# Attention and two MLPs on one core: the rotated q and k split in fewer VectorE steps, and new numbers for the planner

## The chip, the cores and the metric

The kernel runs on one core of one Trainium2 chip. The metric is the time of the whole program on the device in microseconds; the median of three runs before the change is 1078.23 us (1077.92 to 1079.2). Engines are named as the profile names them: PE is TensorE (PEld its weight loads), DVE is VectorE, ACT is ScalarE, POOL is GpSimd, SP is SyncE, whose queue issues the kernel's DMAs.

## The reference

Attention with rotary positions over four batches of eight heads, 576 tokens and a head size of 64, then two dense MLPs over the 2304 tokens (512 to 2048 to 512), the first with x times sigmoid(1.702 x), the second with ELU:

```python
q_rot, k_rot = rotate(q), rotate(k)
scores = (1 / sqrt(D)) * q_rot @ k_rot.T          # (4, 8, 576, 576)
attn = softmax(scores)                            # exp(s - max) / (sum + 1e-9)
x = (attn @ v) in rows of tokens                  # (2304, 512)
h = x @ w_in;  x = (h * sigmoid(1.702 * h)) @ w_out
h = x @ w_in2; out = where(h > 0, h, exp(min(h, 0)) - 1) @ w_out2
```

All inputs are float32 (the weights come as 64-bit numbers that the kernel itself turns into float32).

## The kernel before

Every product is made from two float16 halves. A float32 value is scaled by a power of two, its high half is the value rounded to float16, its low half is what remains. A product takes three matmuls in the MLPs (high times high, high times low, low times high). For the scores, one column of the transposed q holds 64 high and 64 low values of a head, and the first matmul takes it against the high values of k twice over, the second against the low values of k over the high half of q and zeros over the low one: two matmuls in place of three.

The work goes by head pairs: 4 batches times 4 pairs are 16 preparations (`prep`, lines 597 to 709). One of them loads q and k of two heads into the only buffer `R`, takes their largest magnitudes (`amax`), spreads them over the partitions through PE (`across`, lines 354 and 364), makes the scales (`scale`, line 621), rotates (`rope_swap`, `rope_cos`, `rope_add`: lines 634, 638, 642), writes the high halves on ACT (`k_hi`, `q_hi`: lines 656, 662) and the low halves on DVE (`low`, line 667: one instruction for each head), all into the float16 tile `n16`, and transposes that tile with one DMA into `qkT` (line 684). `scale` makes, in DVE steps of two columns, the limited maximum, its exponent bits, the scale `qk_s` and the inverse `qk_i` (lines 336, 338, 340), and the factor of the scores `qk_c` as inverse times inverse times 1/8 (line 626).

A unit of scores is 128 queries of one head (or 64 of two): matmuls (line 798), the maximum on DVE (802), small steps (806, 817, 821), the exponential on ACT (810), the high half on ACT, sometimes on DVE (826, 830), the low half on DVE (838), and a transposing DMA into `et` (844, 847). There are 144 units. When a block of 256 or 320 tokens of a head pair has its transposes, PE multiplies by v (`av`, line 990), ACT and DVE write the halves of `x` (993, 997).

The first MLP (`first_mlp`, lines 1036 and 1070) runs over 8 such blocks; a block can begin when `x` of its four head pairs is there. The second MLP (lines 1177 and 1218) follows when all of the first is done. The weights are turned into float32 in steps on ACT and DVE (lines 424 to 443, the choice of engine free for some), measured (457), and split into halves (500 to 524).

What sets the order is a planner, `Plan.run`: each operation has keys, costs by engine, operations that it must follow and buffers that it needs; each planned engine takes the ready operation with the smallest key, and the instructions are written out in that order for each engine's queue. The keys come from the table `TUNE`; `f_dve` and `f_act` are offsets that bias operations that may run on either engine. MLP work has keys far behind all attention work, so that it fills what PE has left. A switch table `FLEX` holds variants that are off (a form of attention without transposes, `fast_unit`, whose constants are made at the start all the same).

Of the kernel before, what the change touches and what calls it, by code (L numbers as in the profile page):

```python
# [16 lines left out]
P = 128  # L17


FLEX = dict(  # L20
    Ehi=1, Elo=0, glo=0, qk=0, pE=0, pW=0, pg=0, dg=0, r0=1, r1=1, r2=0, r3=0, nt0=0, nt1=0, nt2=0, nt3=0,
)
# [4 lines left out]
    pe_w1i=12, pe_w1o=0, lsame=218.42826132665004, tab=-72.97, f_dve=158.19, f_act=8.42, f_pool=12.224437399728332,  # L27
    w2s=195.33, w1i2=50.4, w1o2=-142.64, dlat=823.3988909607715, qh=-59.5,
    kt=-32.02, vam=131.57, p0=1, lat=344.9241913205742, slack=1000000000.0, w1i=-51.38,
    w1i_s=2.9, w1o=59.09, w1o_s=1.19, prep0_s=0.45, nt=5.6622832505119804,  # L30
    s_f=40.3256386921686, mx_f=6.7540349396707375, ex_f=7.075547533776429, av_f=14.806376760777082, prep0=49.34,
    prep=-60.31, va0=-39.21, va=-62.78, vs=0.59, tiny=2.79,
    av=4.76, ex=-62.15, mx=-22.0, s=-24.23, tr=-61.89,
    bits=-42.89,
# [190 lines left out]
def kernel(  # L225
# [90 lines left out]
    buf("V", ap_, [P, 650], F32, BUFS["V"])  # L316
    buf("mr", ap_, [6, 256], BF16, BUFS["mr"])
# [68 lines left out]
    class Weight:  # L386
        def __init__(self, tile_fn, src, wide, tag, rbuf, key, after=()):
# [107 lines left out]
            for i, c in enumerate(seq):  # L495
                ks = key(16 + i) + TUNE.get(tag + "2", 0.0)

                def hi(e, c=c, i=i):
                    if e == "act":
                        nc.scalar.activation(out=self.h[:, self.at[c], 0:512], in_=self.t[:, i + SP, :], func=AF.Copy, scale=self.sc["s"])  # L500
                    elif e == "pool":
                        nc.gpsimd.tensor_scalar(out=self.h[:, self.at[c], 0:512], in0=self.t[:, i + SP, :], scalar1=self.sc["s"], scalar2=1.0, op0=ALU.mult, op1=ALU.mult)
                    else:
                        nc.vector.tensor_scalar(out=self.h[:, self.at[c], 0:512], in0=self.t[:, i + SP, :], scalar1=self.sc["s"], scalar2=None, op0=ALU.mult)
# [5 lines left out]
                o2 = op({"act": c_act(512, ptr=1), "dve": c_dve(512, 2, ptr=1), **({"pool": 750} if FLEX["pW"] else {})}, hi, [so, free.get(i)], ks, port=True)  # L510
# [63 lines left out]
    def light(e):  # L574
        for a in range(2):
            nc.gpsimd.memset(n16[:, 4 + a, :, D - D * a:2 * D - D * a], 0.0)
        nc.gpsimd.memset(ones, 1.0)
        nc.gpsimd.memset(line, 0.0)
        nc.gpsimd.memset(line[:, D:D + 1], 1e-9)
        nc.gpsimd.memset(square, 1.0)  # L580

    def consts(e):
        nc.gpsimd.tensor_scalar(out=minus, in0=eye, scalar1=-1.0, scalar2=1.0, op0=ALU.mult, op1=ALU.mult)
        nc.gpsimd.tensor_scalar(out=eye16, in0=eye, scalar1=1.0, scalar2=1.0, op0=ALU.mult, op1=ALU.mult)
        nc.vector.tensor_reduce(out=pick_c, in_=eye[0:6, 0:6].rearrange("p (a s) -> p a s", a=2), axis=AX.X, op=ALU.add)
        for a in range(2):
            nc.gpsimd.tensor_scalar(out=pick[:, a], in0=eye[0:6], scalar1=0.0, scalar2=pick_c[:, a:a + 1], op0=ALU.mult, op1=ALU.add)
# [3 lines left out]
    ready_c = op({"pool": 1400}, consts, [begin], key=TUNE["tab"])  # L591
# [5 lines left out]
    def prep(b, hp):  # L597
# [46 lines left out]
        def q_parts():  # L644
            f = take(hN).rearrange("p x j c -> p (x j c)")
            hi = f[:, 0:2 * 704].rearrange("p (h r) -> p h r", h=2)[:, :, 0:640].rearrange("p h (j c) -> p h j c", c=P)[:, :, :, 0:D]
            lo = f[:, D:D + 2 * 576].rearrange("p (h g d) -> p h g d", h=2, g=9)[:, :, 0:9:2]
            return hi, lo

        def k_parts():  # L650
            N16 = take(hN)
            hi = N16[:, 2:4].rearrange("p x j (u d) -> p (x j) u d", u=2)
            return hi, N16[:, 2:4, :, 0:D], [N16[:, 4 + a, :, D * a:D * a + D] for a in range(2)]

        def k_hi(e):
            nc.scalar.activation(
                out=k_parts()[0], in_=R5()[:, 1].rearrange("p h j d -> p (h j) d").unsqueeze(2).to_broadcast([P, 10, 2, D]),
# [3 lines left out]
        def q_hi(e):  # L661
            nc.scalar.activation(out=q_parts()[0], in_=R5()[:, 0], func=AF.Copy, scale=st["s"][:, 0:1])

        def low(e, t, dst, hi):
            for h in range(2):
                if e == "dve":
                    nc.vector.scalar_tensor_tensor(out=dst[h], in0=R5()[:, t, h], scalar=st["s"][:, t:t + 1], in1=hi[:, h], op0=ALU.mult, op1=ALU.subtract)  # L667
                else:
                    nc.gpsimd.tensor_tensor(out=dst[h], in0=R5()[:, t, h], in1=hi[:, h], op=ALU.subtract)

# [650 lines left out]
```

## Time and profile before

| | us |
|---|---|
| median of 3 runs | 1078.23 |
| profiled execution, whole time | 1078.97 |
| its span | 1077.2 |
| PE busy | 964.2 |
| DVE busy | 791.0 |
| ACT busy | 655.0 |

The page gives sums of busy time by engine; PE's share is 90%. A share over the whole says little here, for the stages differ: the attention stage loads all engines, and in the second MLP DVE and ACT wait for PE for long times. The views by stretches and by waits are read for that reason.

### The profile page before, as it was taken

The numbers are of one execution on the slowest core, as the hardware profiler recorded it, in microseconds if no ns is written. First come the engines' busy times: TensorE is split into PE (matmuls) and PEld (weight loads), VectorE is DVE, ScalarE is ACT, GpSimd is POOL, SyncE is SP. The second block draws the span as 40 slices with busy tenths as digits, with TensorE's granted clock in tenths as the row PEclk, the third lists the DMA queues.
The fourth block names the chain that finished last, engine by engine and source line by source line (L and its number), as shares of the span: only waits on it lengthen the run. The fifth ranks groups of instructions, "written<-read, shape, count | busy, mean of one in ns | idle before, by whom it ended". The sixth has DMA issues, their size and how long they took to land.

```text
span 1077.2 us, 18378 instructions
## 1 busy us (share of the span) xinstructions
PE 964.2 (90%) x6710; PEld 612.2 (57%) x6710; DVE 791.0 (73%) x1886; ACT 655.0 (61%) x1277; POOL 8.2 (1%) x31
## 2 busy tenths in 40 slices
PE   1366557999999999999999999999999999999998
PEld 0124325767776767866788778744444444444474
DVE  6998898989989989999895979898066056046051
ACT  5688987868878868877575749675044044035041
POOL 1000000000000000000000000000000000000000
PEclk9998758999999999999999999999999999999999
DMA  8989975488879677876865552711001100000000
GB/s 268 262 202 222 230 163 100 91 177 147 163 162 161 138 165 164 158 157 114 154 123 139 168 164 85 235 58 49 20 10 30 30 11 10 30 10 1 21 20 19
DMA packets 292314, 124.81 MB, mean 116 GB/s; under 512 B 264576, under 2 KB 279552, under 8 KB 292224
## 3 DMA queue, kind: packets, MB, share of 16 engines
q1 hardware_dynamic: 292224, 123.64, 50.6%
q8 instruction: 52, 0.85, 0.4%
q14 instruction: 38, 0.31, 0.1%
HBM read 53.35 MB, written 9.44 MB: 58 GB/s over the span
## 4 chain that ended last, share of the span: by engine, by line
PE 52%; DVE 25%; DMA 11%; ACT 5%; issue 3%; SPq 3%; POOL 0%; DVEq 0%; ACTq 0%; POOLq 0%
PE m L1218 16%; PE m L1177 14%; PE m L1070 9%; DMA et<-Ehl 6%; PE m L1036 6%; PE av L990 4%; DVE Ehl L838 3%; DMA R<-in_k_dram 3%; PE s L798 3%; DVE st L802 3%; DVE t L1043 2%; DVE gl L1053 2%; DVE n L667 2%; ACT E L810 1%; DVE T L634 1%
## 5 line engine op out<-in xcount | busy, mean ns | idle before, releaser
L1036 PE MATMUL m<-x,wi 128*128 128x320 f16 (+1 forms) x1536 | 198.1, 286 | 1.8 <-ACT y L1076 0.9
L1070 PE MATMUL m<-gh,wo 128*128 128x256 f16 (+1 forms) x1024 | 198.5, 286 | 0.0
L1218 PE MATMUL m<-w2o,g 128*128 128x512 f16 x864 | 189.1, 379 | 1.4 <-ACT w2o L500 0.8
L1177 PE MATMUL m<-yhl,w2i 128*128 128x512 f16 (+1 forms) x960 | 188.2, 358 | 2.2 <-DVE e L1188 2.1
L1036 PEld LDWEIGHTS <-wi 128*128 128x128 f16 x1536 | 148.7, 98 | 42.4 <-issue 5.4
L1070 PEld LDWEIGHTS <-wo 128*128 128x128 f16 x1536 | 148.5, 98 | 40.2 <-issue 3.5
L1177 PEld LDWEIGHTS <-w2i 128*128 128x128 f16 x960 | 93.7, 98 | 94.9 <-issue 2.9
L1070 PE MATMUL m<-gl,wo 128*128 128x320 f16 (+1 forms) x512 | 146.3, 286 | 0.0
L1218 PEld LDWEIGHTS <-g 128*128 128x128 f16 x864 | 84.1, 98 | 102.5 <-issue 2.7
L810 ACT ACTIVATE E<-s,st,qk_c 128x576 f32<-128x576 f32 x144 | 118.7, 825 | 23.4 <-DVE st L806 17.4
L798 PE MATMUL s<-qkT 128*128 128x288 f16 (+1 forms) x640 | 102.2, 310 | 27.1 <-ACT E L810 24.5
L838 DVE SCALAR_TENSOR_TENSOR Ehl<-E,st,Ehl 128x576 f16<-128x576 f32 x144 | 116.1, 810 | 10.6 <-ACT Ehl L826 10.1
L826 ACT ACTIVATE Ehl<-E,st 128x576 f16<-128x576 f32 x127 | 97.2, 770 | 36.1 <-DMA et<-Ehl 19.6
L1184 DVE TENSOR_SCALAR e<-e 128x512 f32<-128x512 f32 (+1 forms) x80 | 31.6, 395 | 113.8 <-ACT e L1180 113.8
L802 DVE TENSOR_REDUCE st<-s 128x1 f32<-128x576 f32 x144 | 106.0, 745 | 4.6 <-PE s L798 4.1
L1221 ACT ACTIVATE o<-m,eo 128x512 f32<-128x512 f32 x18 | 12.4, 688 | 158.3 <-PE m L1218 158.3
L798 PEld LDWEIGHTS <-qkT 128*128 128x128 f16 (+1 forms) x640 | 58.0, 105 | 65.3 <-issue 48.0
L1191 ACT ACTIVATE g<-e,y_c 128x512 f16<-128x512 f32 (+1 forms) x80 | 54.2, 677 | 57.5 <-DVE e L1188 57.1
L1195 DVE SCALAR_TENSOR_TENSOR g<-e,y_c,g 128x512 f16<-128x512 f32 (+1 forms) x80 | 55.5, 694 | 28.3 <-ACT g L1191 27.5
L1039 ACT ACTIVATE t<-m,hsc 128x320 f32<-128x320 f32 (+1 forms) x128 | 63.4, 496 | 10.2 <-PE m L1036 9.7
L1180 ACT ACTIVATE e<-m,y_c 128x512 f32<-128x512 f32 (+1 forms) x80 | 50.8, 635 | 22.6 <-PE m L1177 19.7
L1047 ACT ACTIVATE gh<-t 128x320 f16<-128x320 f32 (+1 forms) x128 | 55.5, 439 | 10.0 <-DVE t L1043 9.7
(162 smaller groups left out, 1104.9 us busy)
## 6 DMA issues: line engine op xcount, KB each, us to landing
R<-in_moe_w_in_dram SPq DMA_DIRECT2D x16, 512.0 KB, 4.2
R<-in_moe_w_out_dram SPq DMA_DIRECT2D x16, 512.0 KB, 4.4
gh<-in_moe_w_in_dram SPq DMA_DIRECT2D x8, 512.0 KB, 4.7
R<-in_q_dram SPq DMA_DIRECT2D x16, 256.0 KB, 2.7
R<-in_k_dram SPq DMA_DIRECT2D x16, 256.0 KB, 3.2
gl<-in_moe_w_in_dram SPq DMA_DIRECT2D x8, 512.0 KB, 5.0
V<-in_v_dram SPq DMA_DIRECT2D x32, 128.0 KB, 3.5
gh<-in_moe_w_out_dram SPq DMA_DIRECT2D x8, 512.0 KB, 4.5
```

The lines of the kernel that those rows point to most:

```text
L798: nc.tensor.matmul(o, X[:, a, t], X[:, 2 + 2 * x + a, cs], start=x == 0, stop=x == 1)
L802: nc.vector.tensor_reduce(out=st["t"][:, 0:1], in_=take(hS)[:, :, 0:NS], axis=AX.XY, op=ALU.max, negate=True)
L810: nc.scalar.activation(out=take(hE).rearrange("p (c f) -> p c f", c=2), in_=take(hS)[:, :, 0:NS], func=AF.Exp, bias=t[:, 1:2], scale=csc[b ...
L826: nc.scalar.activation(out=X16[:, 0:S], in_=take(hE), func=AF.Copy, scale=st["t"][:, 3:4])
L838: nc.vector.scalar_tensor_tensor(out=X16[:, S:2 * S], in0=E, scalar=r, in1=X16[:, 0:S], op0=ALU.mult, op1=ALU.subtract)
L1036: nc.tensor.matmul(ps[:, 0:N], W1i.lhs(kk, u, wl), x[:, xl, 0:N], start=kk == 0 and i == 0, stop=kk == KD - 1 and i == 2)
L1039: nc.scalar.activation(out=take(ht)[:, 0:N], in_=take(hM)[:, 0:N], func=AF.Tanh, scale=hsc[b][:, 1:2])
L1047: nc.scalar.activation(out=gh[:, u, 0:N], in_=take(ht)[:, 0:N], func=AF.Copy, scale=DOWN / 2)
L1070: nc.tensor.matmul(ps[:, 0:N], W1o.lhs(f, d, wl), (gh, gl)[xl][:, f, 0:N], start=f == 0 and i == 0, stop=f == KF - 1 and i == 2)
L1177: nc.tensor.matmul(ps[:, 0:n], W2i.lhs(kk, u, wl), Y[:, xl, kk, 0:n], start=kk == 0 and i == 0, stop=kk == KD - 1 and i == 2)
L1195: nc.vector.scalar_tensor_tensor(out=g[:, u, 512:512 + n], in0=take(he)[:, 0:n], scalar=st["c"][:, 1:2], in1=g[:, u, 0:n], op0=ALU.mult, o ...
L1218: nc.tensor.matmul(ps, g[:, f, 512 * gi + P * tt:512 * gi + P * tt + P], W2o.h[:, f, 512 * wl:512 * wl + 512], start=f == 0 and i == 0, st ...
```

## The change

Four things are edited.

- The low halves of q, and those of k, become one DVE instruction of 640 elements for both heads. For that the tile has new columns: both heads of q have their high half in columns 0 to 63 and their low half in 64 to 127, and the low half of k stands in columns 0 to 63 for both heads, with zeros in 64 to 127 (before, the second head had it the other way round).
- The factor of the scores is made by adding exponent bits as integers, from the masked maxima; the inverse scale of q and k is not made any more. The lower limit of the maxima is 2^-47 in place of 2^-60.
- The table of switches and the variants that were off are removed, with their constants (`eye16`, `pick`, `line`), and v's tile has rows of 64 values in place of 65.
- The planner gets other numbers: a smaller cost for the low halves and for `scale`, and most keys in `TUNE`.

```diff
@@ TUNE (two lines of it)
-    kt=-32.02, vam=131.57, p0=1, lat=344.9241913205742, slack=1000000000.0, w1i=-51.38,
+    kt=-23.72, vam=107.88, p0=1, lat=344.9241913205742, slack=1000000000.0, w1i=-85.68,
...
@@ light, consts
-        for a in range(2):
-            nc.gpsimd.memset(n16[:, 4 + a, :, D - D * a:2 * D - D * a], 0.0)
+        nc.gpsimd.memset(n16[:, 4:6, :, D:2 * D], 0.0)
...
-        nc.gpsimd.tensor_scalar(out=eye16, in0=eye, scalar1=1.0, scalar2=1.0, op0=ALU.mult, op1=ALU.mult)
-        nc.vector.tensor_reduce(out=pick_c, in_=eye[0:6, 0:6].rearrange("p (a s) -> p a s", a=2), axis=AX.X, op=ALU.add)
...
@@ scale
-            nc.vector.tensor_scalar(out=m, in0=take(hG)[:, 256:258], scalar1=TINY, scalar2=None, op0=ALU.max)
-            s, inv = scale_bits(m, 2, "qk", 8)
-            c = tiny(1, "qk_c", B * NP)
-            nc.vector.scalar_tensor_tensor(out=c, in0=inv[:, 0:1], scalar=1.0 / D ** 0.5, in1=inv[:, 1:2], op0=ALU.mult, op1=ALU.mult)
...
+            nc.vector.tensor_scalar(out=m, in0=take(hG)[:, 256:258], scalar1=2.0 ** -47, scalar2=None, op0=ALU.max)
+            x = tiny(2, "qk_x", 2, I32)
+            nc.vector.tensor_scalar(out=x, in0=m.bitcast(I32), scalar1=0x7F800000, scalar2=None, op0=ALU.bitwise_and)
+            s = st["s"] = tiny(2, "qk_s", 8)
+            nc.vector.tensor_scalar(out=s.bitcast(I32), in0=x, scalar1=-1, scalar2=268 << 23, op0=ALU.mult, op1=ALU.add)
+            c = csc[b, hp] = tiny(1, "qk_c", B * NP)
+            nc.vector.scalar_tensor_tensor(out=c.bitcast(I32), in0=x[:, 0:1], scalar=-(158 << 23), in1=x[:, 1:2], op0=ALU.add, op1=ALU.add)
...
@@ halves of q and k
+        def part(x, w):
+            return take(hN)[:, x:x + 2, :, D * w:D * w + D].rearrange("p x j d -> p (x j) d")
...
-        def low(e, t, dst, hi):
-            for h in range(2):
-                if e == "dve":
-                    nc.vector.scalar_tensor_tensor(out=dst[h], in0=R5()[:, t, h], scalar=st["s"][:, t:t + 1], in1=hi[:, h], op0=ALU.mult, op1=ALU.subtract)
...
+        def low(e, t):
+            nc.vector.scalar_tensor_tensor(
+                out=part(4 * t, 1 - t), in0=R5()[:, t].rearrange("p h j d -> p (h j) d"), scalar=st["s"][:, t:t + 1],
+                in1=part(2 * t, 0), op0=ALU.mult, op1=ALU.subtract,
+            )
...
-            kl = op({"dve": c_dve(640, k=2, ptr=2)}, k_lo, [kh], key, use=[hR, hN], port=True)
+        kl = op({"dve": c_dve(640, ptr=1)}, k_lo, [kh], key, use=[hR, hN], port=True)
...
@@ v
-    buf("V", ap_, [P, 650], F32, BUFS["V"])
+    buf("V", ap_, [P, 640], F32, BUFS["V"])
```

Where instructions stand now is shown at three places. In these rows `gh` and `gl` are buffers of raw weights, `wi` and `wo` the first MLP's weights, `R` the loaded q and k, `n` the float16 tile, `tab` the rotary table.

SyncE's queue at the program's start, before:

```order
L571 DMA eye<-in_rope_dram 128x128
L572 DMA tab<-in_rope_dram 128x640
L417 DMA gh<-in_moe_w_in_dram 128x1024
L610 DMA R_101<-in_q_dram 128x2x256
L611 DMA R_101<-in_q_dram 64x2x64
L610 DMA R_101<-in_k_dram 128x2x256
L611 DMA R_101<-in_k_dram 64x2x64
```

And after:

```order
L560 DMA eye<-in_rope_dram 128x128
L561 DMA tab<-in_rope_dram 128x640
L413 DMA gh<-in_moe_w_in_dram 128x1024 x2
L413 DMA gl<-in_moe_w_in_dram 128x1024 x2
L592 DMA R_103<-in_q_dram 128x2x256
L593 DMA R_103<-in_q_dram 64x2x64
L592 DMA R_103<-in_k_dram 128x2x256
L593 DMA R_103<-in_k_dram 64x2x64
```

Four loads of weights stand ahead of the first q and k where one stood.

DVE's queue at the first head pair's scale and low halves (`qk_m` to `n`), before:

```order
L623 TENSOR_SCALAR qk_m<-m_130 128x2
L336 TENSOR_SCALAR qk_b<-qk_m 128x2
L338 TENSOR_SCALAR qk_s<-qk_b 128x2
L340 TENSOR_SCALAR qk_i<-qk_b 128x2
L626 SCALAR_TENSOR_TENSOR qk_c<-qk_i 128x1
L642 TENSOR_TENSOR R_101<-R_101,T_121 128x1280
L438 SCALAR_TENSOR_TENSOR gh<-wi,gh 128x512
L438 SCALAR_TENSOR_TENSOR gl<-wi,gl 128x512
L443 SCALAR_TENSOR_TENSOR wi<-wi,gh 128x512
L667 SCALAR_TENSOR_TENSOR n_73<-R_101,qk_s,n_73 128x5x64 x2
L443 SCALAR_TENSOR_TENSOR wi<-wi,gl 128x512
L667 SCALAR_TENSOR_TENSOR n_73<-R_101,qk_s,n_73 128x5x64 x2
```

And after, the scale and what follows it, then (from the third row of the second piece) the low halves:

```order
L605 TENSOR_SCALAR qk_m<-m_146 128x2
L607 TENSOR_SCALAR qk_x<-qk_m 128x2
L609 TENSOR_SCALAR qk_s<-qk_x 128x2
L611 SCALAR_TENSOR_TENSOR qk_c<-qk_x 128x1
L434 SCALAR_TENSOR_TENSOR gh<-wi,gh 128x512
L621 TENSOR_TENSOR R_103<-R_103,tab 128x1280
```

```order
L434 SCALAR_TENSOR_TENSOR gl<-wi,gl 128x512
L439 SCALAR_TENSOR_TENSOR wi<-wi,gl 128x512
L640 SCALAR_TENSOR_TENSOR n_73<-R_103,qk_s,n_73 128x10x64
L429 TENSOR_SCALAR gh<-gh 128x512
L640 SCALAR_TENSOR_TENSOR n_73<-R_103,qk_s,n_73 128x10x64
```

The scale has four steps where it had five, the low halves two instructions where they had four, and more weight steps stand around them.

DVE's queue at the first GELU step of the first MLP (`t<-t,m`; `x` is a half of the attention's result, `Ehl` the halves of the probabilities), before:

```order
L634 TENSOR_TENSOR T_1276<-R_1232,tab 128x20x32
L997 SCALAR_TENSOR_TENSOR x_1512<-av_1468,x_1512 128x256
L508 SCALAR_TENSOR_TENSOR wo<-wo,w1o_s 128x512
L821 RECIPROCAL st<-st 128x1
L838 SCALAR_TENSOR_TENSOR Ehl_1515<-E_1457,st,Ehl_1515 128x576
L771 SCALAR_TENSOR_TENSOR v_1531<-V_697,v_s,v_1531 128x640
L1043 SCALAR_TENSOR_TENSOR t_1550<-t_1550,m_1517 128x320
```

And after:

```order
L502 SCALAR_TENSOR_TENSOR wo<-wo,w1o_s 128x512
L828 SCALAR_TENSOR_TENSOR x_1469<-av_1429,x_1469 128x256
L775 RECIPROCAL st<-st 128x1
L760 TENSOR_TENSOR st<-st,qk_c 128x1
L725 SCALAR_TENSOR_TENSOR v_1472<-V_481,v_s,v_1472 128x640
L502 SCALAR_TENSOR_TENSOR wo<-wo,w1o_s 128x512
L874 SCALAR_TENSOR_TENSOR t_1509<-t_1509,m_1474 128x320
```

The step keeps its neighbours: the sixth result of the attention (the second `x` of 256 columns) stands just ahead of it in both, and one unit of scores fewer stands ahead of it in the order after. PE's queue has the same instructions in both kernels, and its first MLP begins behind 33 units of scores in place of 34.

## Rows read from the trace of the kernel before

**Rows 1.** The page, first part: busy us, share of span, instructions, by engine

```profile
PE 964.2 (90%) x6710; PEld 612.2 (57%) x6710; DVE 791.0 (73%) x1886; ACT 655.0 (61%) x1277; POOL 8.2 (1%) x31
```

**Rows 2.** Busy time by engine in stretches of the span, with columns named

```profile
core 0: us, PE busy (x) PEld busy (x) DVE busy (x) ACT busy (x) POOL busy (x), PEclk, DMA share, GB/s
0.00:60.00 60.00, 14.97 (x108) 8.17 (x108) 49.10 (x104) 39.91 (x70) 3.71 (x18) 1.00 0.96 265
60.00:175.90 115.90, 72.44 (x418) 40.19 (x418) 102.22 (x267) 96.58 (x184) 1.46 (x3) 0.76 0.89 189
175.90:565.50 389.60, 372.55 (x3265) 281.54 (x3263) 357.63 (x958) 299.17 (x624) 3.06 (x10) 1.00 0.73 146
565.50:700.20 134.70, 134.70 (x1123) 106.75 (x1121) 112.58 (x227) 88.11 (x188) 0.00 (x0) 1.00 0.53 158
```

**Rows 3.** PE's waits, 175.9 to 565.5 us: total us, times, longest us

```profile
PE av L990 <- DMA et<-Ehl: 6.8, 8, 1.7
PE s L798 <- ACT E L810: 5.4, 12, 1.0
PE s L798 <- DMA qkT<-n: 2.3, 2, 1.2
```

**Rows 4.** Timeline of PE at the first MLP's start: start us, us, instructions

```profile
167.90 2.83 PE L990 MATMUL av<-et,v 128*64 128x320 f16 x19 [0.45 <-DMA et<-Ehl]
170.31 1.48 PE L990 MATMUL av<-et,vsh 128*64 128x320 f16 x8
173.13 0.65 PE L798 MATMUL s<-qkT 128*128 128x288 f16 x4 [1.34 <-ACT E L810]
...
175.36 0.66 PE L798 MATMUL s<-qkT 128*128 128x288 f16 x4
175.86 5.05 PE L1036 MATMUL m<-x,wi 128*128 128x320 f16 x36
```

**Rows 5.** Groups of DVE instructions by form: count, busy us, mean ns, idle before

```profile
L667 DVE SCALAR_TENSOR_TENSOR n<-R,qk_s,n 128x320 f16<-128x320 f32 x64 | 31.8, 542 | 0.4 <-ACT n L656 0.4
...
L771 DVE SCALAR_TENSOR_TENSOR v<-V,v_s,v 128x640 f16<-128x640 f32 x16 | 13.9, 874 | 0.0
...
L426 DVE TENSOR_SCALAR w2o<-R 128x512 f32<-128x512 f32 x4 | 1.7, 424 | 0.5 <-DMA R<-in_moe_w_out_dram 0.5
L619 DVE TENSOR_REDUCE am<-R 128x2 f32<-128x1280 f32 x1 | 1.5, 1478 | 0.0
...
L433 DVE TENSOR_SCALAR gh<-gh 128x512 int32<-128x512 int32 x2 | 0.9, 428 | 5.3 <-DMA gh<-in_moe_w_in_dram 5.3
...
L524 DVE CAST wi<-m 128x512 f16<-128x512 f32 x1 | 0.7, 673 | 0.0
...
L504 DVE TENSOR_SCALAR wi<-wi,w1i_s 128x512 f16<-128x512 f32 x1 | 0.5, 487 | 0.0
```

**Rows 6.** Timeline of DVE at one scale, one pair of low halves, v's low half

```profile
30.61 0.17 DVE L338 TENSOR_SCALAR qk_s<-qk_b 128x2 int32<-128x2 int32 x1
30.69 0.16 DVE L340 TENSOR_SCALAR qk_i<-qk_b 128x2 int32<-128x2 int32 x1
30.89 0.16 DVE L626 SCALAR_TENSOR_TENSOR qk_c<-qk_i 128x1 f32<-128x1 f32 x1
30.96 1.48 DVE L642 TENSOR_TENSOR R<-R,T 128x1280 f32<-128x1280 f32 x1
...
69.79 0.99 DVE L667 SCALAR_TENSOR_TENSOR n<-R,qk_s,n 128x320 f16<-128x320 f32 x2
70.71 0.14 DVE L806 TENSOR_TENSOR st<-st,qk_c 128x1 f32<-128x1 f32 x1
...
145.56 0.88 DVE L771 SCALAR_TENSOR_TENSOR v<-V,v_s,v 128x640 f16<-128x640 f32 x1
146.35 0.81 DVE L838 SCALAR_TENSOR_TENSOR Ehl<-E,st,Ehl 128x576 f16<-128x576 f32 x1
```

**Rows 7.** DMA issues by line: count, KB each, median us from issue to landing

```profile
gh<-in_moe_w_in_dram SPq DMA_DIRECT2D x8, 512.0 KB, 4.7
```

More of the change, by code (lines that the diff above doesn't have):

```diff
@@ L642, in rope_add @@
             ENG[e].tensor_tensor(out=R, in0=R, in1=take(hT).rearrange("p a j d -> p (a j d)"), op=ALU.add)
[L644 to L653, printed above, removed]
+        def part(x, w):
+            return take(hN)[:, x:x + 2, :, D * w:D * w + D].rearrange("p x j d -> p (x j) d")
         def k_hi(e):
             nc.scalar.activation(
-                out=k_parts()[0], in_=R5()[:, 1].rearrange("p h j d -> p (h j) d").unsqueeze(2).to_broadcast([P, 10, 2, D]),
+                out=take(hN)[:, 2:4].rearrange("p x j (u d) -> p (x j) u d", u=2), in_=R5()[:, 1].rearrange("p h j d -> p (h j) d").unsqueeze(2).to_broadcast([P, 10, 2, D]),
                 func=AF.Copy, scale=st["s"][:, 1:2],
@@ L661, in q_hi @@
         def q_hi(e):
-            nc.scalar.activation(out=q_parts()[0], in_=R5()[:, 0], func=AF.Copy, scale=st["s"][:, 0:1])
-        def low(e, t, dst, hi):
-            for h in range(2):
-                if e == "dve":
-                    nc.vector.scalar_tensor_tensor(out=dst[h], in0=R5()[:, t, h], scalar=st["s"][:, t:t + 1], in1=hi[:, h], op0=ALU.mult, op1=ALU.subtract)
-                else:
-                    nc.gpsimd.tensor_tensor(out=dst[h], in0=R5()[:, t, h], in1=hi[:, h], op=ALU.subtract)
-        def scaled(e, t):
-            x = take(hR)[:, 640 * t:640 * t + 640]
-            nc.gpsimd.tensor_scalar(out=x, in0=x, scalar1=st["s"][:, t:t + 1], scalar2=1.0, op0=ALU.mult, op1=ALU.mult)
+            nc.scalar.activation(out=part(0, 0), in_=R5()[:, 0].rearrange("p h j d -> p (h j) d"), func=AF.Copy, scale=st["s"][:, 0:1])
+        def low(e, t):
[3 more added lines that the diff above has]
+            )
         def k_lo(e):
-            _, hi, lo = k_parts()
-            low(e, 1, lo, hi)
+            low(e, 1)
         def q_lo(e):
-            hi, lo = q_parts()
-            low(e, 0, [lo[:, a] for a in range(2)], hi)
+            low(e, 0)
         def tr(e):
@@ L690, in prep @@
         rd = am_last[hp % 2] = across(lambda: am_t[hp % 2], 2, hG, [am], key)
-        sc = op({"dve": 720}, scale, [rd], key, use=[hG], port=True)
+        sc = op({"dve": 560}, scale, [rd], key, use=[hG], port=True)
         reng = lambda n: {"dve": c_dve(n)}
@@ L719 @@
     v_loaded = {}
-    n_fast = sum(FLEX[f"nt{hp}"] for hp in range(NP))
-    def fast(n, hp):
-        b, chunks, tail, n0, N = blocks[n]
-        return n == 0 and len(chunks) == 2 and not tail and FLEX[f"nt{hp}"]
     def v_view(b, hp):
-        return take(("vs", b, hp)).rearrange("p (a d) -> p a d", d=D + 1)
+        return take(("vs", b, hp)).rearrange("p (a d) -> p a d", d=D)
     def v_prep(b):
@@ L1257 @@
                 s_unit(i, trs, trs_st)
-            (fast_unit if fast(n, hp) else av_unit)(n, hp, trs, trs_st)
+            av_unit(n, hp, trs, trs_st)
     prev = None
```

155 lines of the change are left out of this document (13 added, 142 removed).

## The prediction, made before the changed kernel ran

> **What bounds the kernel now.** I read the page's engine totals first [rows 1]: PE is busy for 964.2 of the span's 1077.2 us, DVE for 791.0, and only 113.0 us of the span are without a matmul. Totals hide the stages, so the next view is the table by stretches [rows 2], cut at 175.9 us, where PE takes up the first MLP's first matmul [rows 4]. PE's idle time there is stretch minus busy: 60.0 - 15.0 = 45.0 us in the first 60 us, 115.9 - 72.4 = 43.5 us up to 175.9, 389.6 - 372.6 = 17.0 us up to 565.5, and none from 565.5 to 700.2. That leaves 113.0 - 105.5 = 7.5 us for the second MLP, which the change doesn't reach except by its weight steps. So the end is "start of the first MLP on PE, plus a fixed amount of PE work, plus the stalls behind it". The change leaves PE's instructions as they are, the same forms and counts. Only two terms can move: when the first MLP starts (call it A0), and the 17.0 us of stalls between A0 and 565.5.
>
> What sets A0? The PE rows ahead of it [rows 4] show no wait at 175.86. It stands in PE's order behind two score steps and another unit's attention product; the last operand that its own block lacked came out of the attention product that went on at 167.90, after a wait for the transposed probabilities, and ended at 170.31 + 1.48 = 171.8. Those probabilities come through DVE (maximum, reciprocal, low half), and DVE is busy for 49.1 of the first 60 us and 102.2 of the next 115.9 [rows 2]: idle 10.9 + 13.7 = 24.6 us in 175.9. (PE's granted clock is 0.76 of full between 60 and 175.9 us and 1.00 behind; with 43.5 us idle there PE isn't the limit at either level, and the change gives no reason for another one behind A0.) DVE's work ahead of A0 is therefore the thing to count. Behind A0 the picture turns: PE 96% busy, DVE 357.6 of 389.6 us (92%), and PE's waits are for the probabilities' transposes, 6.8 us, for ScalarE's exponentials that free a score buffer, 5.4 us, and for the transposed q and k, 2.3 us [rows 3]. The first two end in a chain through DVE too, so less DVE work can shorten them, but no further than their sum.
>
> **The merged low halves.** Before, the low half of q or k is two instructions of 320 elements, 64 in all, 542 ns each [rows 5]. They are pipelined: a pair that begins at 69.79 lets the next instruction start at 70.71, 0.92 us on [rows 6]. After, one instruction of 640 elements. The nearest row is v's low half: same operation, types and size, 874 ns [rows 5], and the instruction behind it starts 146.35 - 145.56 = 0.79 us on [rows 6]. Gain 0.13 us a pair, 0.26 us for each of the 16 head pairs. The new output is strided (64 of every 128 columns) where v's is not; the old pairs wrote with the same kind of stride, and 2 x 542 against 874 bounds the gain at 0.21 us a pair; no row excludes a loss, which I bound by zero gain. I take 0.13.
>
> [...]
>
> **The scale by exponents.** Before, five small steps in a chain [rows 6]: s starts at 30.61, the inverse at 30.69, the product that waits for the inverse at 30.89, the next large step at 30.96. The step behind a step that it needs starts 0.20 us on, the step that needs nothing of its neighbour 0.07 to 0.08. After there are four: the product needs the masked exponents, not its neighbour. One 0.20 falls out, 0.2 us a head pair. The larger lower bound on the maxima changes no time. The third edit, the keys' columns, only moves where the zeros lie, and the ScalarE steps keep their sizes.
>
> **What the new numbers of the planner move.** Ahead of the first GELU step in DVE's order, five head pairs have their low halves and six their scales in both kernels: 5 x 0.26 + 6 x 0.2 = 2.5 us less. But the engine choice moves work the other way. On DVE there, by the order: four more shifts of weights (428 ns), two more conversions of wo (424 ns), two more maxima of v (no row; half of the 1478 ns maximum of q and k, 0.74): 1.71 + 0.85 + 1.48 = 4.0 us more; a cast (673 ns) and two high halves (487 ns, and as much for the second) fewer: 1.6 us less [rows 5]. Net +2.4, which eats the gain of the merge. What else stands ahead of that point differs by one unit of scores (its maximum, low half and small steps, 2.0 us), one low half of wo (0.75) and the one reduction of six rows that is dropped (0.15) fewer, and one cosine product (1.48) and one high half (0.52) more: -0.9. Sum at A0: -2.5 + 2.4 - 0.9 = **-1.0 us**. ScalarE, which gives those steps away, has room: busy 136.5 of 175.9 us [rows 2].
>
> Behind A0 the rest of the savings lies: 11 x 0.26 + 10 x 0.2 = 4.9 us, and the one maximum of q and k that DVE had taken (1478 ns) goes to ScalarE; the 0.9 us shifted ahead comes back: 4.9 + 1.5 - 0.9 = 5.5 us less of DVE's 357.6. Its worth lies between nothing (PE runs at 96% and fills DVE's slack with MLP work) and 5.5 us, never over 14.5 us, the three waits [rows 3]. I take 2.0, a good third, since PE's own work is nearer to the limit here than DVE's.
>
> **The start.** In SyncE's queue four loads of w_in now stand ahead of the first q and k, and up to the second q and k twelve instead of seven: DVE converts w_in first, and the first score's maximum has some 9 us more DVE work ahead of it. By the seventh score unit that is regained, since w_in is then done. I cost it at nothing in the sum: DVE has weight work in place of the head pair's, and where a load is late there, it idles as it does now (10.9 us in the first 60, at least 4.7 of it the first landing). If loads fall further behind, that cover is gone (rival 3). The dropped GpSimd constants ran beside the first load.
>
> **The sum.** -1.0 - 2.0 = -3.0 us. The profiled execution took 1078.97 us, 1.77 of it around the span; it would take 1076.0. It lies 0.74 us above the median of 1078.23, on whose scale the forecast is **1075.2 us**.
>
> **Rivals.**
> 1. The freed DVE time is hidden: MLP matmuls fill PE, the stalls stay, and the moved conversions eat the rest. For it: PE's 96%. Against: 14.5 us of its waits run through DVE or its transposes. With A0's 1.0 us alone, or half of that, 1077.7.
> 2. It gives more: w_in ready early means that PE's and DVE's gaps ahead of A0 close. Before, DVE's idle time there is 24.6 us, at least 4.7 of it the first load's landing [rows 7]; a quarter of the other 19.9 is 5.0 us. For it: the start of the MLP has one score unit fewer ahead of it. Against: DVE's waits ahead of A0 are scattered. With 1.2 us more from the stalls: 1075.2 - 5.0 - 1.2 = 1069.0.
> 3. Slower: the start becomes bound by loads. The first 60 us already move 265 GB/s with the DMA engines 96% busy [rows 2]. By their shapes, what lies ahead of and with the second q and k is twelve weight loads of 0.524 MB, two sets of q and k of 0.59, three of v of 0.33 and 0.39 of tables, 8.84 MB: 33.4 us at that rate. DVE's work ahead of their use, some 26 us by the order, behind a first load that takes 4.7 us to land [rows 7], ends at about 31. It is that close, and the weight loads wait for one of four buffers; two landings laid open are 9.4 us, of which I count 6.5, since DVE has some of the work already. The sum becomes +3.5: 1081.7. It turns the sign past 0.2% when DVE's idle time in the first 60 us passes 10.9 + 5.2 us. Against it: now the loads, in another order, leave only 10.9 - 4.7 = 6.2 us of idle time there.
>
> That the transposed q and k come too late also speaks for slower: the new order has a few head pairs prepared with less work between them and their first scores. The waits for them are two now, 2.3 us, the longest 1.2 [rows 3]; three more of 1.2 us would cost 3.6 and leave +0.6, which is within what I call no change.
>
> **How the numbers follow.** Forecast 0.50, rival 1 0.19, rival 2 0.12, rival 3 0.19. About what a measurement of this kernel can tell from no change is 0.2%, 2.2 us: of the forecast's 0.50 I put 0.38 beyond it and 0.12 within (an A0 gain of nothing, or 1 us of stalls). Faster 0.38 + 0.12 = 0.50; within 0.12 + 0.19 = 0.31; slower 0.19. The range reaches from rival 2 to nearly rival 3, 1069.0 to 1081.0: its upper end is where 5.8 us of added idle time at the start leave +2.8. Faster and not faster hold about the same; the forecast's own range is 1073.0 (both terms 2.1 us better) to 1077.2 (stalls unchanged).
>
> **What would show it.** Low halves at 32 of about 874 ns, starting about 0.79 us before their successor; the inverse gone. A0 near 175 us; PE idle behind it, up to 565, near 15 instead of 17.0; DVE busy some 6 us less in the whole. PE's totals within 1 us. The term of the start is wrong if DVE idles over 16 us in the first 60, the second term if the waits for exponentials and transposes sum to 14.5 again, and the count by work ahead if A0 moves by over 3 us.

## The result, and the profile after

| | before | after |
|---|---|---|
| median of 5 runs, us | 1079.20 | 1086.99 |
| profiled execution, whole time | 1078.97 | 1089.56 |
| its span | 1077.2 | 1087.8 |
| PE / DVE / ACT busy | 964.2 / 791.0 / 655.0 | 968.8 / 788.3 / 649.2 |

The ratio is 1.0079 (95% interval 1.0051 to 1.0106): the change costs 0.8%, where 1075.2 us and a range up to 1081.0 were forecast. The stretches of after, with the columns of [rows 2], cut at its own first MLP matmul:

```profile
0.00:60.00 60.00, 16.62 (x109) 9.45 (x111) 47.74 (x99) 37.73 (x65) 3.43 (x12) 0.99 0.93 267
60.00:175.00 115.00, 71.01 (x413) 37.02 (x410) 103.18 (x255) 93.84 (x178) 0.92 (x3) 0.67 0.91 187
175.00:565.50 390.50, 370.76 (x3221) 279.14 (x3219) 350.83 (x922) 299.76 (x629) 3.06 (x10) 1.00 0.79 146
565.50:700.20 134.70, 132.41 (x1137) 106.75 (x1135) 109.19 (x227) 83.39 (x181) 0.00 (x0) 1.00 0.50 149
```

Stretch minus PE busy gives the account. The first MLP starts 0.9 us earlier (175.00 for 175.86). PE idles behind that start for 19.7 us up to 565.5 (before 17.0 [rows 2]), then 2.3 (before none), then 9.6 in the rest (119.0 in all less 87.4, 19.7 and 2.3; before 7.4): 7.1 us more. And PE's busy time behind A0 is 968.8 - 87.6 = 881.2 for 876.8 us: 4.4 more for the same matmuls. -0.9 + 7.1 + 4.4 = 10.6, the difference of the spans.

The 2.7 us up to 565.5 hide a larger shift. Cut at 340, PE idles 5.2 us ahead of it (before 10.0) and 14.6 behind it (before 7.0). PE's waits from 340 to 565.5 (total us, times, longest), after and then before:

```profile
PE s L752 <- ACT E L764: 7.3, 12, 1.9
PE av L821 <- DMA et<-Ehl: 5.1, 5, 1.4
PE m L867 <- DVE t L874: 1.9, 4, 1.4
```

```profile
PE s L798 <- ACT E L810: 2.5, 5, 1.0
PE s L798 <- DMA qkT<-n: 2.3, 2, 1.2
PE av L990 <- DMA et<-Ehl: 1.7, 1, 1.7
```

In this pair of executions the 4.4 us are mostly clock. Behind A0 the granted clock was 1.00 throughout in before, also in stretches of 4 us; after has two dips, each behind a stall of PE (stretches of after, same columns; the clock is the third number from the end):

```profile
505.00:511.00 6.00, 4.37 (x33) 3.04 (x32) 3.12 (x11) 1.78 (x4) 0.00 (x0) 1.00 1.05 141
511.00:515.00 4.00, 3.59 (x17) 2.22 (x17) 4.00 (x10) 3.15 (x7) 0.00 (x0) 0.66 0.76 156
515.00:519.00 4.00, 4.00 (x42) 2.67 (x41) 3.08 (x10) 2.41 (x6) 0.00 (x0) 0.91 0.39 76
720.00:727.00 7.00, 7.00 (x26) 2.80 (x24) 5.71 (x13) 4.32 (x8) 0.00 (x0) 0.76 0.00 0
```

The mean of 0.66 is made up of 0.99 up to 512.3 and 0.50 from 512.5 to 515.5; the matmuls of `wo` start 0.27 us apart there (513.54 and 513.81) and 0.14 ahead of the wait (508.93 and 509.07), at 1.00. So a busy us is taken to do the clock's share of its work, and as an estimate from these rows the three short stretches lose 3.59 x 0.34 + 4.00 x 0.09 + 7.00 x 0.24 = 3.3 us. The second dip follows two waits at the joint of the MLPs, where the maxima of its weights and of its input go through DVE (1.8 and 1.8 us, with only two small matmuls of that step between them). But such dips don't mark the new order. The merge in the old order (below), faster than before, has them too: its mean clock is 0.96 from 240 to 280 us and 0.94 from 700 to 730, where before's is 1.00, and its 37.86 and 27.50 busy us there lose some 3 us by the same working. Before's execution happened to have none.

### One stall, followed back

Where does the wait for the exponentials come from? The longest one, 1.94 us at 511.31, in four timelines of after (start, us, engine, line, operation, idle time before it and who ended it):

```profile
499.04 5.55 SPq L652 DMA_TRANSPOSE qkT<-n  x1
505.03 3.76 SPq L795 DMA_TRANSPOSE et<-Ehl  x2
508.88 2.55 SPq L792 DMA_TRANSPOSE et<-Ehl  x2
```

```profile
503.51 0.76 ACT L780 ACTIVATE Ehl<-E,st 128x576 f16<-128x576 f32 x1
504.18 0.82 ACT L764 ACTIVATE E<-s,st,qk_c 128x576 f32<-128x576 f32 x1
...
509.67 0.78 ACT L780 ACTIVATE Ehl<-E,st 128x576 f16<-128x576 f32 x1 [4.22 <-DMA et<-Ehl]
510.35 0.81 ACT L764 ACTIVATE E<-s,st,qk_c 128x576 f32<-128x576 f32 x1
```

```profile
507.49 0.14 DVE L760 TENSOR_TENSOR st<-st,qk_c 128x1 f32<-128x1 f32 x1
510.48 0.82 DVE L786 SCALAR_TENSOR_TENSOR Ehl<-E,st,Ehl 128x576 f16<-128x576 f32 x1 [2.85 <-ACT Ehl L780]
```

```profile
511.31 0.65 PE L752 MATMUL s<-qkT 128*128 128x288 f16 x4 [1.94 <-ACT E L764]
```

Read from the top: the transposing of q and k holds SyncE's queue for 5.55 us. The probabilities' transposes behind it start at 505.03. A buffer of split probabilities (`Ehl`, three of them) is free again only when its transpose has landed, so ScalarE's next high half waits 4.22 us. Behind that high half stand the exponential that frees a score buffer and, on DVE, the low half (2.85 us idle). PE waits 1.94 us for the score buffer, and then the clock falls (0.50 from 512.5 to 515.5). ScalarE's waits for the buffer that end at 385.6, 478.1, 540.9 and 544.1 us (2.4 to 4.1 us) stand in the same place, each behind a transposing of q and k that began 10 to 13 us earlier; with this one they make 16.2 of its 19.5 us of such waits between 340 and 565.5. Before has these holds of the queue too (4.6 to 5.4 us each); there the waits are 9.9 us.

### The profile page after: what moved, and what is told of

The parts are those of the page before. It is cut to its first block, busy times and chain, and to the rows that moved or that the text cites. A ratio compares the mean times of both kernels' runs of the same rounds, so it can differ in the third digit from the quotient of the medians.

```text
span 1087.8 us, 18313 instructions
## 1 busy us (share of the span) xinstructions
PE 968.8 (89%) x6710; PEld 611.7 (56%) x6710; DVE 788.3 (72%) x1845; ACT 649.2 (60%) x1270; POOL 7.4 (1%) x25
## 4 chain that ended last, share of the span: by engine, by line
PE 45%; DVE 22%; DMA 13%; ACT 6%; issue 4%; SPq 2%; ACTq 0%; DVEq 0%; POOL 0%
PE m L1049 16%; PE m L1008 14%; DMA et<-Ehl 6%; PE m L901 5%; PE m L867 4%; DVE Ehl L786 3%; DVE st L756 3%; PE av L821 3%; PE s L752 2%; DMA qkT<-n 2%; DVE t L874 2%; DVE gl L884 2%; ACT Ehl L780 2%; DMA R<-in_moe_w_out_dram 1%; DMA R<-in_moe_w_in_dram 1%
## 5 line engine op out<-in xcount | busy, mean ns | idle before, releaser
L1052 ACT ACTIVATE o<-m,eo 128x512 f32<-128x512 f32 x18 | 12.4, 687 | 162.6 <-PE m L1049 162.6
```

## The experiments

Theory and rivals changed as results came in; each expectation was written before its run. The ratio is to the kernel before, run on the same chip.

### Is it the place of the tiles, the merge, or the order?

Without the dropped constants, most large tiles of after begin 128 bytes past a multiple of 256 in their partition; most of before's begin at one. One pad moves them back in after, and away in before.

```diff
-    ones = ap_.tile([P, 1], BF16, name="ones")
+    ones = ap_.tile([P, 80], BF16, name="ones")[:, 0:1]
```

> The changed kernel with one constant tile made 128 bytes larger, so that all attention tiles behind it start at multiples of 256 bytes of a partition, as most did before the change; no instruction moves. Theory P (place): removing the constants had shifted the tiles by 128 bytes against 256, each transposing DMA takes longer to land, the probabilities' buffers come free later. Then the median landing of the probabilities' transposes in 340 to 565 us falls from 3.3 to 2.9-3.0, ACT's wait for them there from 19.5 to about 10 us, and the time from 1087 to 1073-1078, ratio to before 0.993 to 0.999. Rival O (order): the planner's new order itself stalls PE; then the time stays 1085-1089, ratio 1.006 to 1.010.

Measured 1088.05, 1.0082 (1.0068 to 1.0095): the place isn't the cause of the loss.

> The kernel before with the same 128 bytes added, which puts its attention tiles at 128 modulo 256 (qkT's first buffer and v's tiles at other remainders, as they were). Same instructions, same order. Theory P: 1086-1091, ratio 1.007 to 1.011, landing of the probabilities' transposes 3.2-3.3 us in the median instead of 2.9-3.0. Rival O: no change, ratio 0.998 to 1.002.

Measured 1083.05, 1.0031 (1.0021 to 1.0042): a small cost in before's order, which neither theory had right.

Then the planner's table alone, `TUNE` of before in after (with the pad), and `TUNE` of after in before.

```diff
-    av=-35.55, ex=-47.09, mx=-17.64, s=-15.34, tr=-66.0,
+    av=4.76, ex=-62.15, mx=-22.0, s=-24.23, tr=-61.89,
...
```

> The changed kernel, tiles at multiples of 256 bytes again, with the planner's TUNE of before: the merged low halves and the scale by exponents alone. Theory P: this and the first run are both faster than before by the merge, ratio 0.995 to 0.999 (1073-1078). Rival O: this one gets the gain of the merge, 0.996, and the first run doesn't.

> The kernel before with the new TUNE only; its tiles stay where they were (multiples of 256 bytes but for the first qkT buffer and v). Theory P: about as before, ratio 0.997 to 1.003. Rival O: the whole loss, ratio 1.006 to 1.012 (the merge, which would take some 0.3% off, is not in it).

Measured 1082.08, 1.0025 (1.0011 to 1.0039), and 1095.47, 1.0148 (1.0129 to 1.0167). With the old table most of the loss is gone, and the new table alone costs more than the whole change. Both theories missed here: they had the first below 1 and the second at 1.012 at most. And the smaller costs that the planner is given for the merged steps move work too, so these two don't isolate the merge. The next two do: they hold the whole order, costs included, to before's and to after's.

```diff
-        sc = op({"dve": 560}, scale, [rd], key, use=[hG], port=True)
+        sc = op({"dve": 720}, scale, [rd], key, use=[hG], port=True)
...
-        kl = op({"dve": c_dve(640, ptr=1)}, k_lo, [kh], key, use=[hR, hN], port=True)
+        kl = op({"dve": c_dve(640, k=2, ptr=2)}, k_lo, [kh], key, use=[hR, hN], port=True)
...
```

> The merge alone, at an order that is held: the changed kernel with the planner's numbers and its three changed costs (low halves, scale, constants) of before, so that every engine and the DMA queue run the list of before, with 64 low halves of 320 columns replaced by 32 of 640, and 16 inverses and the unused constants gone; the tiles lie at the same places as before. Theory O (the merge helps, the new order costs): the working of the prediction without the moved steps, 2.5 us earlier at the first MLP's start and a third of the 4.9 us behind it, 1079.3 - 2.5 - 1.7 = 1075, ratio 0.996 (0.993 to 0.998). Rival W (the freed VectorE time is worth nothing, since an earlier start only turns into longer stalls behind it): 1079.3, ratio 0.999 to 1.001.

> The new order alone: the kernel before with the planner's numbers and three changed costs of after, so that every engine and the DMA queue run the list of after, but with the low halves in pairs of 320 columns and the old scale chain. Theory O: the changed kernel at this place of tiles took 1088.05; the pairs and the inverse cost 16 x 0.46 = 7.4 us of VectorE again, of which a half or more shows, as this stage waits for VectorE: 1092, ratio 1.012 (1.010 to 1.015). Rival W: 1088, ratio 1.008, as the changed kernel. Were the merge itself the loss and the order harmless, it would be near 1080.

Measured 1077.61, 0.9985 (0.9973 to 0.9998), and 1089.62, 1.0089 (1.0073 to 1.0104). Against the whole change at the same place of tiles (1.0082), the four corners say: the new order costs 0.9 to 1.0%, with or without the merge; merge, scale chain and dropped constants together give 0.15% in the old order and 0.07% in the new, 1.6 and 0.8 us. In the old order that is less than theory O had (0.2 to 0.7%), in the new order nothing that can be measured, as rival W had it.

### Which of the numbers?

Three groups of `TUNE` were set back in after (with the pad), one at a time: the attention units' keys, the keys of loads and weights, and `f_dve`, `f_act`.

> The changed kernel (tiles placed as before) with six of the numbers set back: the keys of the attention units (scores, maximum, exponential, transpose, attention product, small steps). Theory K (the loss lies in how far ahead the exponentials, high halves and transposes of the units run): most of the loss of 8.8 us goes, 1080 to 1083, and ScalarE's waits for a free buffer of split probabilities between 340 and 565 us go back from 19.5 to about 10 us. Rival G (the engine choice of the conversions) or rival B (the times of loads and weights): 1086 to 1090, unchanged.

> The changed kernel (tiles placed as before) with eighteen of the numbers set back: when loads, preparations and weight conversions are due. Rival B (the new due times of loads and weights cost): 1080 to 1083. Theory K (the attention units' keys) and rival G (the engine choice): 1085 to 1091. If this and the attention units' keys set back, each by itself, both leave 1085 or more, the loss sits in their combination or in the two offsets of the engine choice.

> The changed kernel (tiles placed as before) with the two numbers set back that say how late VectorE and ScalarE take steps that either could do. Setting back the attention units' keys gave 1.0051, the eighteen load and weight numbers 1.0139, all of them 1.0025. Rival G (the engine choice of the conversions carries the loss): 1080 to 1083, and VectorE's busy time in the whole falls by 3 us or more. If the loss sits in how the three groups fit together: 1086 to 1093, no better than the changed kernel.

Measured 1085.39, 1.0051 (1.0031 to 1.0072); 1095.19, 1.0139 (1.0123 to 1.0154); 1102.95, 1.0212 (1.0189 to 1.0235). No group carries the loss alone. With the attention keys set back ScalarE's waits for a buffer did fall to 9.4 us, as theory K said, but little more than a third of the loss went with them (1.0051 against 1.0082, intervals that touch). The two others came out slower than any theory had them. They made the joint of the MLPs worse; PE's longest waits behind 565.5 there, for the load keys and then for the offsets:

```profile
PE m L350 <- DVE y_a L970: 10.8, 1, 10.8
```

```profile
PE m L350 <- DVE y_a L970: 12.7, 1, 12.7
```

A number of this table is worth something only beside the others.

### Is the buffer the mechanism?

Here the order stays word for word and the split probabilities get a fourth buffer, taken in turn.

```diff
+            if p == "Ehl":
+                i = turn["Ehl"] = (turn["Ehl"] + 1) % 4
...
-    junk = per.tile([P, 640], F16, name="junk")
+    junk = per.tile([P, 640], mybir.dt.uint8, name="junk")
```

> The changed kernel (tiles placed at multiples of 256 bytes) with four buffers instead of three for the split probabilities, taken in turn, at exactly its own order on every engine and on the DMA queue; the space comes from a scratch output of ScalarE that is kept in bytes. Theory H (each transposing of q and k holds the DMA queue for about 5 us; the probabilities' transposes behind it come late, ScalarE's next high half waits for a buffer, VectorE's low half for that, PE for scores and products): ScalarE's waits for a free buffer between 340 and 565 us fall from 23.8 to under 8 us, PE's idle time behind the first MLP's start up to 565 from 19.2 to 11 to 15 us, and the time from 1088 to 1080 to 1084. Rival S (the units are late by the order, and the buffer is only where the lateness shows; with another buffer the exponentials or the score buffers wait instead): ScalarE's waits for a buffer fall too, but PE's idle time stays within 2 us of 19.2 and the time at 1086 to 1089.

> The merge in before's order, as the run that held the order (1077.61), with four buffers for the split probabilities. Theory H: that order has the same holds of the DMA queue, but fewer of them reach PE (PE idle 14.0 us behind the first MLP's start up to 565); 1 to 3 us of it go, 1074.5 to 1076.5, faster than either kernel. Rival S: 1077 to 1078, as without.

Measured 1080.13, 1.0005 (0.9985 to 1.0025), and 1074.24, 0.9955 (0.9937 to 0.9974). With the new order the buffer takes back 8 us; with the old order it makes a kernel faster than both. ScalarE's and DVE's waits on this chain and PE's idle time, new order, three buffers and then four (waits from 340 to 565.5 us, stretches from A0):

```profile
ACT Ehl L780 <- DMA et<-Ehl: 23.8, 10, 4.7
DVE Ehl L786 <- ACT Ehl L780: 15.7, 12, 3.3
```

```profile
175.20:565.50 390.30, 371.11 (x3248) 280.08 (x3247) 352.79 (x930) 301.63 (x634) 3.06 (x10) 1.00 0.72 147
```

```profile
ACT Ehl L783 <- DMA et<-Ehl: 4.0, 2, 2.5
DVE Ehl L789 <- ACT Ehl L783: 2.0, 3, 1.0
```

```profile
173.00:565.50 392.50, 380.07 (x3308) 287.13 (x3306) 359.78 (x949) 307.29 (x645) 3.06 (x10) 0.99 0.74 148
```

The waits go, and PE's idle time falls from 19.2 to 12.4 us. The scratch kept in bytes costs ScalarE nothing: 737 ns a step in the median either way. Theory H holds: this part of the loss passes through these buffers. That the transposing of q and k is what holds them is read from the timelines above; no run issues the two kinds apart.

The buffers aren't the whole difference between the orders, for the old order gains 3.4 us by the fourth one and stays 5.9 us ahead. The same stretch with the old order and the merge, three buffers and then four:

```profile
175.04:565.50 390.46, 376.49 (x3301) 285.64 (x3299) 358.68 (x936) 303.13 (x634) 3.07 (x10) 1.00 0.73 147
172.80:565.50 392.70, 378.90 (x3319) 287.18 (x3318) 360.03 (x942) 305.05 (x641) 3.06 (x10) 1.00 0.73 146
```

With three buffers the new order's span is 9.9 us longer (1085.3 and 1075.4, profiled executions, both with the merge): 5.2 us are PE's idle time in this stretch (19.2 and 14.0), 3.2 its idle time behind 565.5 (10.9 and 7.7), 1.3 its busy time behind A0. With four, the new order idles even less in this stretch (12.4 and 13.8). It stays 4.3 us longer (1077.7 and 1073.4) by 2.9 us of idle time behind 565.5 (10.9 and 8.0) and 2.7 us of busy time. That idle time is the joint of the MLPs, where the new order waits three times and the old one once (PE's waits of over 1 us behind 565.5, four buffers, new order and then old):

```profile
PE m L363 <- DVE y_a L973: 1.8, 1, 1.8
PE m L353 <- DVE e L1022: 1.8, 1, 1.8
PE m L353 <- DVE y_a L973: 1.6, 1, 1.6
```

```profile
PE m L1011 <- DVE e L1022: 2.4, 1, 2.4
```

So about half of the order's cost passes through the buffers, and about a third is the joint.

### What is VectorE's time worth?

The prediction's rates would give the merge and the scale chain 4 us; they gave 1.6. So the merge alone was undone, with four buffers and with three, at before's order.

```diff
-            nc.vector.scalar_tensor_tensor(
-                out=part(4 * t, 1 - t), in0=R5()[:, t].rearrange("p h j d -> p (h j) d"), scalar=st["s"][:, t:t + 1],
-                in1=part(2 * t, 0), op0=ALU.mult, op1=ALU.subtract,
-            )
+            for h in range(2):
+                nc.vector.scalar_tensor_tensor(
+                    out=part(4 * t, 1 - t)[:, 5 * h:5 * h + 5], in0=R5()[:, t, h], scalar=st["s"][:, t:t + 1],
...
```

> The merge undone alone, where the buffers no longer bind: the run with before's order and four buffers for the split probabilities (1074.24, ratio 0.9955), but with each low half of 640 columns written as two steps of 320 again, 64 for 32; the scale chain, the layout of the tile and every other step stay. By the trace the pairs cost 32 x 0.13 = 4.2 us of VectorE more, 1.3 us of it ahead of the first MLP's start. Theory F (the merge was hidden by the waits for buffers, and is worth its VectorE time once they are gone): 1077 to 1078.5, ratio 0.997 to 0.9985. Rival C (the merge is worth the 1.6 us that it gave with three buffers, and the buffers' gain is a separate one): 1075 to 1076, ratio 0.9965. If it stays at 1074 the merge is worth nothing and the buffer did all.

> The merge undone alone, with three buffers: the run that held before's order (1077.61, ratio 0.9985), with each low half of 640 columns written as two steps of 320 again; scale chain, layout of the tile and all other steps stay. If the merge gave that run its 1.6 us: 1079 to 1080, ratio 0.9995 to 1.0005. If the merge is worth nothing here either and the 1.6 us came from the shorter scale chain and the constants that are gone: 1077 to 1078, ratio 0.9975 to 0.999.

Measured 1073.18, 0.9944 (0.9924 to 0.9964), and 1079.27, 0.9990 (0.9976 to 1.0003): against 0.9955 and 0.9985 with the merge, nothing that can be measured, either way. Larger doses were needed: the low halves written twice, only k's twice (this edit), or left out for all but the first head pair, in the last case with both numbers of buffers.

```diff
         def k_lo(e):
             low(e, 1)
+            low(e, 1)
```

> The suspected cost doubled: the run that held before's order, with each of the 32 low halves of q and k written twice, 32 x 0.79 = 25 us of VectorE more, all in front of the transposing of q and k, 10 of them ahead of the first MLP's start. By the prediction's rates (all of the time ahead of that start counts, a third to two fifths behind it): 7.9 + 0.37 x 17.4 = 14 us more, 1092, ratio 1.011 to 1.014. If VectorE's time has slack in nearly every stage: 2 to 5 us more, ratio 1.000 to 1.003. One us of VectorE per us would be 1103.

> Half the dose: the run that held before's order with only k's 16 low halves written twice, 12.6 us of VectorE more. Theory R: 0.85 x 12.6 = 10.7 us more, 1088, ratio 1.007 to 1.010. Theory T: less than half of the full dose's 21.2 us, 2 to 8 us, ratio 1.001 to 1.006.

> The suspected cost taken away: the run that held before's order (1077.61, ratio 0.9985), with the low halves of q and k left out but for the first head pair (the later pairs multiply stale low parts), 30 x 0.79 = 23.7 us of VectorE less at the same order. The dose of 25 us more cost 21.2 us, 0.85 per us. Theory R (VectorE's time counts at that rate in both directions): 1057 to 1060, ratio 0.979 to 0.983. Theory T (it is a limit only when it grows; below the present load the buffers, the transposes and TensorE's own work set the pace): 1070 to 1076, ratio 0.991 to 0.997.

> The same with four buffers for the split probabilities (with low halves 1074.24, ratio 0.9955); low halves of q and k left out but for the first head pair. Theory R: 1053 to 1056, ratio 0.976 to 0.979. Theory T, with the buffers as the next limit: the gain is larger than with three buffers by 2 us or more, 1064 to 1070; with TensorE or the transposes as the next limit it is the same few us, 1068 to 1073.

| VectorE time changed by, us | ratio (interval) | against the run without that dose | per us |
|---|---|---|---|
| +25.2 | 1.0179 (1.0157 to 1.0202) | +1.94%, 20.9 us | 0.83 |
| +12.6 | 1.0071 (1.0052 to 1.0091) | +0.86%, 9.3 us | 0.74 |
| +4.2 (pairs) | 0.9990 (0.9976 to 1.0003) | +0.05%, 0.5 us | not to be told from 0 |
| -23.7 | 0.9933 (0.9913 to 0.9953) | -0.52%, 5.6 us | 0.24 |
| -23.7, four buffers | 0.9877 (0.9857 to 0.9896) | -0.78%, 8.4 us | 0.35 |

The first column counts low halves at 0.79 us each (0.13 for a pair); VectorE's busy totals moved by +25.4, +11.9, +2.9, -20.7 and -20.2 us. Time added costs 0.74 to 0.83 of itself, time taken away gives a quarter to a third. Theory T had the second part right. The added time it had too cheap: the half dose (1.0071) fell into theory R's range, outside T's 1.001 to 1.006, and the full dose cost more than the prediction's rates give (1.011 to 1.014).

These halves stand right ahead of the transposing of q and k, so a late transposing is a rival to VectorE's load. The traces speak against it: with the full dose PE's waits for that transposing between 175 and 565.5 us go from 2.0 to 2.6 us, those for the exponentials from 1.9 to 12.8. The last low half of the probabilities, without and with the full dose (ns min/median/max, first and last start):

```profile
L786 DVE SCALAR_TENSOR_TENSOR Ehl<-E,st,Ehl x144: 785/811/820, 43.0 to 571.9; 128x576 f16<-128x576 f32 x144
```

```profile
L787 DVE SCALAR_TENSOR_TENSOR Ehl<-E,st,Ehl x144: 786/812/820, 45.2 to 592.4; 128x576 f16<-128x576 f32 x144
```

Attention ends 20.5 us later for 25.2 us of work. In the other direction the other waits grow. From 175 to 565.5 us, with the low halves and without them, three buffers each:

```profile
ACT Ehl L780 <- DMA et<-Ehl: 12.7, 8, 3.3
DVE Ehl L786 <- ACT Ehl L780: 6.5, 10, 1.2
DVE st L771 <- ACT E L764: 5.1, 12, 1.0
```

```profile
ACT Ehl L782 <- DMA et<-Ehl: 16.6, 9, 3.6
DVE st L773 <- ACT E L766: 11.0, 21, 1.1
DVE Ehl L788 <- ACT Ehl L782: 10.9, 15, 2.2
```

The last two of these waits of DVE, both for ScalarE, rise by 10.3 us together: that much of the freed time is spent there. Why the pairs' 4.2 us cost less than the larger doses' rate, which would be 2 to 3 us, isn't settled.

## Why the prediction was wrong

- **The low halves and the scale: right.** 32 of 877 ns in the median; one starts at 387.87 and its successor at 388.66, 0.79 us on. In the scale chain the product now starts 0.08 us behind the scale, as forecast.

```profile
381.01 0.17 DVE L609 TENSOR_SCALAR qk_s<-qk_x 128x2 int32<-128x2 int32 x1
381.09 0.15 DVE L611 SCALAR_TENSOR_TENSOR qk_c<-qk_x 128x1 int32<-128x1 int32 x1
381.16 0.16 DVE L775 RECIPROCAL st<-st 128x1 f32<-128x1 f32 x1
...
387.87 0.88 DVE L640 SCALAR_TENSOR_TENSOR n<-R,qk_s,n 128x640 f16<-128x640 f32 x1
388.66 0.15 DVE L760 TENSOR_TENSOR st<-st,qk_c 128x1 f32<-128x1 f32 x1
```

- **A0: right in size** (175.00, forecast near 175), but with luck. The count itself has an error: one more maximum of v stands ahead of the first GELU step, not two (at 30.55 us; the other comes at 325.6), so its sum is -1.7, not -1.0. And it is no count to rely on. At before's order, where the count says -2.5, A0 was 175.0 too; 7.9 us of low halves more moved it by 4.6; the pairs, 1.3 us more by count, by 3.5 with three buffers.
- **The sum "A0 plus PE work plus stalls" failed.** A gain at A0 need not last. Before with the new table starts the first MLP at 170.4, 5.4 us earlier, and is 1.5% slower; PE then idles 26.9 us up to 565.5, where before idled 17.0.
- **The stalls behind A0: the first step that failed.** The prediction put the worth of 5.5 us of VectorE "between nothing ... and 5.5 us" and took 2.0. It counted how much work the new order leaves behind A0, not where it stands, and so excluded a loss there. Idle time was 19.7 us where 15 was forecast, and the three waits sum to 16.5 us (7.5, 7.3 and 1.7) where 14.5 would already have told against the term. The order costs 0.9 to 1.0%, about half of it by way of the buffers of split probabilities, which come free late. Against the forecast's -2.0 these stalls rose by 2.7: 4.7 of the 13.6 us between the forecast and this execution's span.
- **The size of freed time was too high as well.** All of it ahead of A0 and a third behind; measured, a quarter over all for the large dose, nothing to be told for the 4.2 us.
- **"PE's totals within 1 us" and "no reason for another clock": wrong.** 4.4 us more behind A0, 3.3 of them in the two dips. They are another third of the miss, but not one that the order explains: at before's order the merge had such dips as well.
- **The second MLP, taken as hardly reached: the second step that failed.** PE idles 4.4 us more behind 565.5 (11.9 for 7.4), the last third of the miss, most of it in three waits at the joint of the MLPs (5.3 us) where before had one (2.1).
- **DVE's total** fell by 2.7 us, not 6.
- **The rivals.** Rival 3 had the sign with the wrong place: DVE idles 60 - 47.7 = 12.3 us in the first 60, below its 16.1, and no slow start shows. Q and k that come too late, which the prediction also names, didn't show either: PE waits for them for 1.7 us behind A0, twice, where it was 2.3. No rival was about the buffers, though [rows 3] showed the wait that ends in them, and the queue in which the transposes stand was in the profile.

## What to carry to other kernels

In this kernel several limits stand close together (PE is busy for 95% and DVE for 90% of the stretch from A0 to 565.5 in after): freeing VectorE's time returned 0.24 to 0.35 per us, with other waits growing in its place (DVE's for ScalarE by 10.3 us), while adding time cost 0.74 to 0.83. So don't read the worth of less work off what more work costs. Price a new order by where its waits fall, not by the amount of work ahead of a point, and hold the order when you want to know what an edit is worth. Look for the buffer that is freed last behind a queue that long issues hold (4.6 to 5.6 us here): one more of `Ehl` gave 0.3% in the old order and 0.8% in the new, more than the merge and the scale chain (0.15%).

## What was not expected of the hardware

**The place of a tile.** With the large tiles 128 bytes off a multiple of 256, the queue kept the DMA engines busier for about the same packets and bytes (80.3% against 73.0%), and the probabilities' transposes took longer to land (3.3 us against 2.9). From 340 to 565.5 us, after as it is and after with the pad (the queue's packets, MB and share of 16 engines; then count and median us from issue to landing):

```profile
q1 hardware_dynamic: 116167, 32.92, 80.3%
...
et<-Ehl SPq DMA_TRANSPOSE x74, 3.3
```

```profile
q1 hardware_dynamic: 116891, 33.03, 73.0%
...
et<-Ehl SPq DMA_TRANSPOSE x75, 2.9
```

In before, moved off by the pad, the share went from 74.0 to 82.3% and the landing from 2.9 to 3.3 us. Why the place does this isn't shown. What it cost in time differed: 0.31% in before, nothing that can be measured in after.

**The hold of the queue.** In after, a transposing of q and k held SyncE's queue for 4.6 to 5.6 us (the issues at 375.59, 467.35, 499.04 and 531.30; the next ones start at 380.29, 472.39, 505.03 and 536.02), one of the probabilities for 1.3 in the median, and nothing behind it was issued meanwhile.

**The clock behind a stall.** In after, PE waits of 1.8 to 1.9 us were followed by stretches at 0.66 and 0.76 of full clock, 4 and 7 us long. Not every wait of about that length was: behind 2.1 us (up to 712.15) and 1.7 us (up to 493.05) in before the clock stayed at 1.00 (from 712.15 to 716.15 and from 493 to 497). What tells them apart isn't shown.
